# Linear attention and a squared-ReLU layer in one kernel: attention cut into smaller slices that are placed by running sums of two engines' work, and strip one's DMAs in another order

## The chip, the cores and the metric

The kernel runs on one core of a Trainium2 chip. The metric is device time in microseconds of that core, as a median over runs. Five engines work side by side, each through its own instructions in order: PE (TensorE, matrix products; its weight loads stand in the profile as an engine of their own, PEld), DVE (VectorE), ACT (ScalarE), POOL (GpSimd) and SP (SyncE), which here issues nearly all DMAs.

## The reference

```python
kv  = np.einsum('bhsd,bhse->bhde', k, v)        # b=8, h=8, s=576, d=64
out = np.einsum('bhsd,bhde->bhse', q, kv)
rms = np.sqrt(np.mean(out * out, axis=-1, keepdims=True) + 1e-06)
x   = (out / rms * g_norm)                      # to 4608 tokens x 512
h   = x @ w_in                                  # 512 -> 2048
y   = (np.maximum(h, 0.0) ** 2) @ w_out         # 2048 -> 512
```

Everything is float32. The two weight matrices arrive in 64 bits.

## The kernel before, in words

**Tokens.** The 4608 tokens are 36 tiles of 128, and nine strips of four tiles (512 tokens). Strips 0 and 1 have their own program, strips 2 to 8 share one. For each strip the feed-forward part has two stages. The up stage makes h and squares it, and the down stage multiplies by `w_out`. From strip 1 on, the products are made by the recursive seven-product scheme for 2x2 block matrices, one level deep in strip 1's up stage, two levels deep elsewhere. So each stage is a row of small matrix products (`up_small`, L1125; `small_products`, L941) whose results are added up by DVE, ACT and POOL.

**An up stage of strips 2 to 8** is 55 slots (`up_slot`, L1096). Seven outer products start seven slots apart, each with seven inner ones two slots apart, so from slot 7 on two of them interleave. An inner product fills one of the PSUM banks A, B, C (`BANK`); A takes four inner products one after the other, and each next one adds to what lies there. Before it does, ACT or DVE must have read the bank: L1155 (ACT copy), L1150 (DVE add), L1163 (ACT copy). The squaring is on ACT, two instructions (L1088, L1089). POOL makes sums of inputs (L288) and of results in SBUF (L1150). In slots 40 to 51 DVE also makes the first operands of the down stage (`leaf_steps`, L918).

**A down stage** is 14 steps. Each outer product there needs two weight blocks from DRAM, 0.75 MB from `w_out` (L831) and 1 MB from `w_deep` (L837). `stream` (L819) loads them in order of use into four equal buffers (`stream_pool`), and the buffers also hold `w_in_deep` blocks for the up stages (L825). Strips 0 and 1 write `w_deep` (L857, L863) and `w_in_deep` (L1051) themselves, from sums that DVE and POOL make; some of these sums lie in the same four buffers, others in the eight of `sum_pool`.

**Attention** for later strips is worked off between these products. `slices` (L630 to L690) is a list written out in order, and `attend` (L692) runs it up to a given place. For a pair of tiles it holds:

- `transposed_query` (L377): one DVE transpose of a query block (L383), for the last block of an odd batch a second one (L387); it also queues the loads of later queries.
- `key_value` (L414): PE products of k and v (L431), two ACT copies (L436, L437).
- `query` (L504): PE products (L467) for both tiles into one PSUM tile `x_ps`, of which there is one; two ACT squares (L476).
- `mean_roots` (L521): two DVE sums (L484), a scale and shift (L485), and ACT's root (L490).
- `normalized` (L527): four small DVE instructions (L495 to L499), and one DVE multiplication of 128x512 for each tile (L535).
- `squares_x` (L598): one DVE transpose for each tile (L602).
- `send_x` (L609): a store to DRAM (L611); `fetch_x` (L614) loads it back in the feature-major order, four DMAs (L618), at least six ticks of a planner's clock later.

**What sets the order.** The main loop (L1188 on) calls one feed-forward step, then perhaps one load, then `attend`. In strips 2 to 8 the list is spread evenly over the first 36 slots (`pace = 36`), one slice at a time and whole. Before strip s the loop calls `attend(ready[s])`, so that everything that strip s needs has been emitted. Loads of keys, of tiles and of queries wait in queues with due times on the planner's clock, which adds 1.2 for each up slot. A query is loaded only after its turn in the list has freed a buffer (three buffers).

**SP's queue** runs in program order. The built program gives its DMAs eight completion semaphores in turn, so a DMA also waits until the eighth before it has landed. A DMA that waits for an engine holds up all behind it.

**Strip 0's end and strip 1.** In strip 0's down stage SP stores `w_out` sums, loads the keys of batch 2 and the strip's last blocks. In strip 1's up stage (28 steps) POOL makes seven `w_in_deep` sums (`deep_sums_in`, L1044), DVE the last `w_deep` sums (in four parts, at steps 7, 9, 11 and 13), and the first four blocks of the down stage are loaded at steps 21, 22, 23 and 25. I call these b0 to b3, and the next ones b4 and so on.

Of the kernel before, what the change touches and what calls it, by code (L numbers as in the profile page):

```python
# [10 lines left out]
FP32 = mybir.dt.float32  # L11
# [3 lines left out]
AF = mybir.ActivationFunctionType  # L15
# [5 lines left out]
def kernel(  # L21
# [47 lines left out]
    NT = 4  # L69
# [4 lines left out]
    DEEP_UP = 2  # L74
    SQ = 32
    Q_ON_PE = 2
    X_ON_PE = 2
    EPS = 1e-6
    const = ctx.enter_context(tc.tile_pool(name="const", bufs=1))
# [207 lines left out]
    def minus(eng, out, a, b):  # L287
        eng.tensor_tensor(out=out, in0=a, in1=b, op=ALU.subtract)  # L288
# [125 lines left out]
    def key_value(b, *ps_of):  # L414
        while any(f == load and a[:2] == (b, p) or f == load_rest and a[0] == b for _, f, a in keys_due for p in ps_of):
            _, f, a = keys_due.popleft()
            f(*a)
        ps = apsum.tile([P, len(ps_of), D], FP32, name="kv_ps", tag="at")
        if (b, ps_of[0]) == (0, 0):
            keep_busy(ps[:, 0], 3)  # L420
            warm = apsum.tile([P, NT, P], FP32, name="x_ps", tag="first")[:, 0]
        half = slice(REST * (b % 2), REST * (b % 2 + 1))
        tiles = [[main.pop((n, b, p)) for n in "kv"] for p in ps_of]
        steps = [(i, c) for i in range(len(ps_of)) for c in range(C)] + [(i, C) for i in range(len(ps_of))]
        for i, c in steps:
            if (b, ps_of[i], c) == (0, 0, C):
                keep_busy(warm, 2)
            for h in range(2):
                at = (slice(None), h, c) if c < C else (half, 2 * ps_of[i] + h)
                a, w = (t[at] for t in (tiles[i] if c < C else (k_rest, v_rest)))  # L430
                nc.tensor.matmul(  # L431
                    ps[ts(h, D), i], lhsT=a, rhs=w, start=i == 0 and c == 0, stop=c == C, skip_group_check=True
                )
        at = (NP * b + ps_of[0]) % (2 * NP)
        d = kv_all[:, at : at + len(ps_of)]
        nc.scalar.copy(d[0:D, :, 0:D], ps[0:D])  # L436
        nc.scalar.copy(d[D:P, :, D:P], ps[D:P])  # L437
        for i, p in enumerate(ps_of):
            kvd[b, p] = d[:, i]
            if b < 2:  # L440
                if b == 1 and p == 0:
                    load_next()
            else:
                u = next(to_load, None)
                if u is not None:
                    keys_later(load, *u, nc.sync, "kv")
                if p == NP - 1 and b + 1 < B:
                    keys_later(load_rest, b + 1, nc.sync)

    by_head = lambda t: t.rearrange("p (h d) -> p h d", d=D)  # L450
# [37 lines left out]
    def root_of(ms, ps=None):  # L488
        r = ps if ps is not None else small.tile([P, 2, H], FP32, name="rms", tag="rms")[:, : ms.shape[1]]
        nc.scalar.activation(r, ms, AF.Sqrt)  # L490
        return r
# [23 lines left out]

    def roots_normalized(ns):
        parts, ms = queried.pop()
        queried.append((parts, (ms, root_of(ms))))
        normalized(ns)

    def mean_roots(ns):  # L521
        parts, sqs = queried.pop()
        ms = mean_of(sqs)
        r = apsum.tile([P, 2, H], FP32, name="root", tag="at")[:, : len(ns)]
        queried.append((parts, (ms, root_of(ms, r))))

    def normalized(ns):  # L527
        parts, means = queried.pop()
        r = inverse_root(*means)
        for i, n in enumerate(ns):  # L530
            x_n[n] = xn_pool.tile([P, d_model], FP32, name="x_n", tag="x_n")
            o = x_n[n].rearrange("p (q r d) -> p r q d", r=2, d=D)
            x = parts[i].rearrange("p r (q d) -> p r q d", d=D)
            w = r[:, i].rearrange("p (r q) -> p r q", r=2).unsqueeze(3).to_broadcast([P, 2, NP, D])
            nc.vector.tensor_tensor(out=o, in0=x, in1=w, op=ALU.mult)  # L535

    first = {}
    TAG_UP = "ABAC"
# [70 lines left out]
    def send_x(n):  # L609
        d = sent[n] = dram.tile([P, 4, NP, SQ], FP32, name="x_d", tag="x_d", bufs=2 * NT)  # L610
        nc.sync.dma_start(out=d, in_=squared.pop(n))  # L611
        tiles_due.append((clock[0] + 6, fetch_x, (n,)))

    def fetch_x(n):  # L614
        s, i = divmod(n, NT)
# [48 lines left out]
    T, K, last = transposed_query, key_value, query_pairs(1)[2]  # L664
    slices += [(query_means, (last,)), (K, (2, 0, 1)), (T, (2, 0)), (roots_normalized, (last,)), (T, (2, 1))]
    slices += [(T, (2, 2)), (features, (last[0],)), (T, (2, 3)), (K, (2, 2, 3))]
    for b in range(2, B):
        pairs = query_pairs(b)
        for i, pair in enumerate(pairs):
            left = len(pairs) - i  # L670
            more = b + 1 < B
            at = left + (b == 2)
            keys = (b + 1, *{2: (0, 1), 1: (2, 3)}[at]) if more and at < 3 else ()
            if i == 0 and b > 2:
                slices += [(T, (b, p)) for p in (2, 3)]
            if i == 0 and b == 3:
                slices.append((K, (3, 2, 3)))
            slices.append((query, (pair, *keys)))
            if more and left == 1:
                slices.append((T, (b + 1, 1)))  # L680
            slices.append((mean_roots, (pair,)))
            slices.append((normalized, (pair,)))
            if more and left == 2:
                slices.append((T, (b + 1, 0)))
            slices += [(squares_x, (n,)) for n in pair]
            for n in pair:
                slices.append((send_x, (n,)))
                if n % NT == NT - 1:
                    ready[n // NT] = len(slices)
    slice_at = [0]  # L690

    def attend(n):  # L692
        while slice_at[0] < min(n, len(slices)):
            fn, a = slices[slice_at[0]]
            fn(*a)
            slice_at[0] += 1

    def out_rows(n):

# [343 lines left out]

    def deep_sums_in(b):  # L1044

        t = stream_pool.tile([P, 4, FQ // 2, P], FP32, name="w_i", tag="w_blk")
        s1, s2, s4 = (t[:, i].rearrange("p f e -> p (f e)").rearrange("p (g e) -> p g e", g=2) for i in range(3))
        nc.gpsimd.tensor_tensor(out=s1, in0=w_half(b, 0, 1), in1=w_half(b, 1, 1), op=ALU.add)  # L1048
        minus(nc.gpsimd, s2, s1, w_half(b, 0, 0))
        minus(nc.gpsimd, s4, w_half(b, 1, 0), s2)  # L1050
        nc.sync.dma_start(  # L1051
            out=w_in_deep[b].rearrange("p n g e -> p n (g e)"), in_=t[:, 0:3].rearrange("p n f e -> p n (f e)")
        )

    def deep_differences_in(b):
# [132 lines left out]
    for s in range(N_STRIP):  # L1188
# [19 lines left out]
        goal, begun = ready.get(s + 1, len(slices)), slice_at[0]  # L1208
        if s >= DEEP_UP:
            goal = max(goal, min(ready[DEEP_UP] + (len(slices) - ready[DEEP_UP]) * (s - 1) // (N_STRIP - DEEP_UP - 1), len(slices)))  # L1210
        total, done = sum(w for w, _, _ in steps), 0
        for i, (w, fn, a) in enumerate(steps):
            if s == 0 and i < n_up:
# [32 lines left out]
            if s:  # L1246
                clock[0] += 3.2 if i >= n_up else 2.2 if s == DEEP else 1.2
                soon = tiles_due and tiles_due[0][2][0] // NT == s + 1
                if i == n_up + 10:
                    while tiles_due and tiles_due[0][2][0] // NT == s + 1:  # L1250
                        _, f, a = tiles_due.popleft()
                        f(*a)
                elif not due(keys_due) and not (soon and due(tiles_due)):
                    least = 2.1 if s == DEEP else 4.5 if i < n_up else 3.3
                    quiet = n_up * 2 // 3 < i < n_up + 3 or s == DEEP and i > n_up + 5
                    if not quiet and clock[0] >= dripped[0] + least:
                        dripped[0] = clock[0]
                        drip(True)
                pace = 25 if s == DEEP else 36
                attend(begun + (goal - begun) * min(i + 1, pace) // pace)  # L1260
                if s == DEEP and i in (7, 9, 11, 13):
                    if i == 7:
                        last_sums = store_deep_sums(*deep_due.popleft())
                    next(last_sums, None)
                if s == DEEP and i == n_up - 3:
                    leaf_sums(s, 4)
                if s == 1 and i in range(2, 23, 3):
                    deep_sums_in((1, 6, 5, 4, 0, 2, 3)[i // 3])
                if s == 1 and i in (21, 22, 23, 25):
                    stream()  # L1270
                continue
            if i == n_up:
# [15 lines left out]
                deque(store_deep_sums(*deep_due.popleft()), 0)  # L1288
            if i == n_up + 2:
                store_first(2)  # L1290
                for _ in range(2):
                    load_next(names="kv")
            if i == n_up + 3:
                load_rest(2, nc.sync)
            if 11 <= i < n_up:

# [31 lines left out]
```

## Time and profile before

| what | value |
|---|---|
| median of 3 runs (lowest, highest) | 898.01 us (897.0, 902.7) |
| the profiled execution: its own time | 897.09 us |
| the profiled execution: its span | 895.0 us |
| granted TensorE clock | 0.999 |
| DMA: bytes moved, mean rate | 235.71 MB, 263 GB/s |

The span runs from the first to the last instruction; 2.1 us of the time lie around it. The ends of matmuls are modelled in this profile, so PE looks busy even when the next product starts late. I therefore read the starts of the products, and the idle time before weight loads (PEld): in a stage of small products, weight loads follow each other without a gap unless the next product has to wait. A timeline row shows start, length, engine, line, what is written and read, how many instructions it merges, and in brackets the idle time before it and who ended it.

In the time line of the two-level stages, one product of the scheme is a row of eight PE instructions, and the next such row starts 0.89 us later. That is also the length of one up slot. One whole outer product of a down stage takes 6.25 us.

### The profile page before, as it was taken

The page shows a single profiled execution, that of the slowest core. Times are in us where ns is not written, and L with a number is a line of the kernel's source. Part 1 is how long each engine was busy: PE and PEld are TensorE (multiplying, and loading weights), DVE is VectorE, ACT ScalarE, POOL GpSimd, SP SyncE. Part 2 cuts the span into 40 slices and gives each one's busy share as a digit, 9 for nine tenths or more (in the row PEclk, how much of TensorE's full clock was granted, in tenths as well). Part 3 has the DMA queues.
Part 4 walks back from the last instruction along what each step waited for, and adds up shares of the span by engine and source line. Part 5 has one row for each costly group of instructions (what it writes and reads, how often), then busy time and mean ns, then how long its engine had stood idle before and what let it go on. Part 6 is the DMA issues. An engine that isn't in the chain of part 4 may idle for free.

```text
span 895.0 us, 20696 instructions
## 1 busy us (share of the span) xinstructions
PE 879.5 (98%) x8296; PEld 822.0 (92%) x8296; DVE 730.9 (82%) x1256; ACT 315.3 (35%) x622; POOL 306.7 (34%) x315
## 2 busy tenths in 40 slices
PE   8999999999999999999999999999999999999998
PEld 7445888889999999999999999999999999999998
DVE  4999988878778986798689966985899778875886
ACT  5898242220027302640255023801271027102710
POOL 0000005700448233731373035604460447044700
PEclk9999999999999999999999999999999999999999
DMA  9998998999988798799886989798748965884384
GB/s 322 317 300 266 290 361 246 260 303 336 309 208 280 261 324 234 189 331 325 249 231 242 320 247 239 244 293 299 218 142 295 302 205 164 301 299 155 127 321 177
DMA packets 169663, 235.71 MB, mean 263 GB/s; under 512 B 79456, under 2 KB 134240, under 8 KB 161248
## 3 DMA queue, kind: packets, MB, share of 16 engines
q1 hardware_dynamic: 169408, 234.40, 81.2%
q8 instruction: 65, 1.06, 0.5%
q14 instruction: 30, 0.25, 0.1%
q10 hardware_dynamic: 160, 0.00, 0.0%
HBM read 197.66 MB, written 36.70 MB: 262 GB/s over the span
## 4 chain that ended last, share of the span: by engine, by line
PE 75%; DVE 12%; DMA 8%; issue 2%; SPq 2%; ACT 1%; DVEq 0%; POOL 0%; POOLq 0%; ACTq 0%
PE ps_B L950 21%; PE ps_A L1138 16%; PE ps_A L950 16%; PE ps_B L1138 8%; PE ps_C L1138 4%; PE ps_A L733 3%; DMA w_blk<-w_deep 2%; DMA w_deep<-w_t 2%; PE kv_ps L431 2%; DVE w_c L268 2%; PE x_ps L467 1%; DVE w_t L288 1%; PE ps_B L733 1%; DMA raw<-in_moe_w_in_dram 1%; DVE wt L288 1%
## 5 line engine op out<-in xcount | busy, mean ns | idle before, releaser
L950 PE MATMUL ps_B<-w_blk,g_s 128*128 128x128 f32 x1024 | 126.2, 275 | 0.0
L950 PEld LDWEIGHTS ps_B<-w_blk,g_s 128*128 128x128 f32 x1024 | 120.0, 192 | 0.2
L1138 PE MATMUL ps_A<-x_l,w_in 128*128 128x128 f32 x784 | 104.1, 276 | 0.0
L950 PE MATMUL ps_B<-w_blk,gt 128*128 128x128 f32 x768 | 97.6, 275 | 2.9 <-DMA w_blk<-w_out 1.7
L288 POOL TENSOR_TENSOR x_l<-xT 128x256 f32<-128x256 f32 x21 | 15.7, 749 | 241.8 <-PE ps_A L950 241.8
L1138 PEld LDWEIGHTS ps_A<-x_l,w_in 128*128 128x128 f32 x784 | 95.4, 192 | 0.5 <-DVE gt L1150 0.2
L950 PEld LDWEIGHTS ps_B<-w_blk,gt 128*128 128x128 f32 x768 | 91.4, 192 | 3.7 <-issue 2.1
L950 PE MATMUL ps_A<-w_blk,g_s 128*128 128x128 f32 x768 | 93.6, 275 | 0.0
L950 PEld LDWEIGHTS ps_A<-w_blk,g_s 128*128 128x128 f32 x768 | 89.6, 192 | 0.0
L1150 POOL TENSOR_TENSOR snap<-snap,gt 128x512 f32<-128x512 f32 x35 | 46.6, 1331 | 119.3 <-ACT snap L1155 49.0
L1155 ACT COPY snap<-ps_A 128x512 f32<-128x512 f32 x63 | 36.7, 582 | 133.6 <-PE ps_A L1138 111.0
L965 DVE TENSOR_TENSOR o_sb<-o_sb,ps_B 128x256 f32<-128x256 f32 (+1 forms) x128 | 49.5, 387 | 33.0 <-ACT o_sb L966 25.9
L1088 ACT ACTIVATE gt<-gt 128x512 f32<-128x512 f32 x112 | 69.6, 622 | 18.0 <-DVE gt L1150 18.0
L950 PE MATMUL ps_A<-w_blk,gt 128*128 128x128 f32 x576 | 72.3, 275 | 0.0
L1089 ACT ACTIVATE gt<-gt 128x512 f32<-128x512 f32 x112 | 70.6, 631 | 3.6
L950 PEld LDWEIGHTS ps_A<-w_blk,gt 128*128 128x128 f32 x576 | 68.2, 192 | 0.0
L1150 POOL TENSOR_TENSOR gt<-gt,snap 128x512 f32<-128x512 f32 x42 | 52.6, 1276 | 23.4 <-DVE snap L1150 23.4
L1048 POOL TENSOR_TENSOR w_i<-w_in 128x512 f32<-128x512 f32 x7 | 9.8, 1396 | 147.2 <-DMA q<-in_q_dram 141.6
L288 DVE TENSOR_TENSOR gt<-gt 128x2048 f32<-128x2048 f32 (+1 forms) x29 | 59.7, 2063 | 0.0
L966 ACT COPY o_sb<-ps_A 128x128 f32<-128x128 f32 x24 | 6.4, 265 | 145.8 <-PE ps_A L950 145.8
L1138 PE MATMUL ps_A<-x_l,w_blk 128*128 128x128 f32 x392 | 52.2, 276 | 1.3 <-issue 1.2
L1138 PE MATMUL ps_B<-x_l,w_blk 128*128 128x128 f32 x392 | 52.0, 276 | 0.0
(180 smaller groups left out, 1805.5 us busy)
## 6 DMA issues: line engine op xcount, KB each, us to landing
w_blk<-w_deep SPq DMA_DIRECT2D x56, 1024.0 KB, 6.9
w_blk<-w_out SPq DMA_DIRECT2D x56, 768.0 KB, 5.9
w_blk<-w_in_deep SPq DMA_DIRECT2D x49, 768.0 KB, 5.2
raw<-in_moe_w_in_dram SPq DMA_DIRECT2D x16, 512.0 KB, 7.6
raw<-in_moe_w_out_dram SPq DMA_DIRECT2D x16, 512.0 KB, 6.8
k<-in_k_dram SPq DMA_DIRECT2D x29, 256.0 KB, 4.6
v<-in_v_dram SPq DMA_DIRECT2D x29, 256.0 KB, 4.9
x_d<-x_q SPq DMA_DIRECT2D x27, 256.0 KB, 5.0
```

What stands on the lines that cost most here:

```text
L268: yield nc.vector.scalar_tensor_tensor(out=ci, in0=high, scalar=-(2**30), in1=ci, op0=ALU.bitwise_and, op1=ALU.bitwise_or)
L288: eng.tensor_tensor(out=out, in0=a, in1=b, op=ALU.subtract)
L431: nc.tensor.matmul(ps[ts(h, D), i], lhsT=a, rhs=w, start=i == 0 and c == 0, stop=c == C, skip_group_check=True)
L733: nc.tensor.matmul(bank[BANK[p]][:, i, :], lhsT=lhsT(k), rhs=rhs(k), start=p in (1, 5, 2) and i == 0 and k == 0, stop=k == n - 1, skip_gro ...
L950: nc.tensor.matmul(chain[c][x][:, i, :], lhsT=a[:, f, :], rhs=w[:, f, :], start=x not in opened[c] and f == 0, stop=f == FQ // 2 - 1, skip ...
L965: add = lambda out, a, b: nc.vector.tensor_tensor(out=out, in0=a, in1=b, op=ALU.add)
L1048: nc.gpsimd.tensor_tensor(out=s1, in0=w_half(b, 0, 1), in1=w_half(b, 1, 1), op=ALU.add)
L1088: nc.scalar.activation(o, o, AF.Relu)
L1089: nc.scalar.activation(o, o, AF.Square)
L1138: nc.tensor.matmul(ps[:, i, :], lhsT=w, rhs=rhs, start=j in (1, 2, 5) and i == 0, stop=True, skip_group_check=True)
L1150: add = lambda eng, out, a, b: eng.tensor_tensor(out=out, in0=a, in1=b, op=ALU.add)
L1155: nc.scalar.copy(t, ps)
```

## The change

1. **Smaller slices from batch 3 on.** `mean_roots` and `normalized` are cut up: `mean` (one tile's sum on DVE), `root` (ACT), `inverse` (four small DVE instructions), and `scaled_heads`. The last takes the place of DVE's multiplication at L535: for half of a tile's heads it gives ACT four multiplications of 128x64, each with a scale per partition. Batch 2 keeps the old slices.
2. **Placement by running sums.** In strips 2 to 8 `attend_between` takes the place of the even spread. It keeps a sum for DVE and one for ACT. Each slot takes 0.9 us off and adds what the feed-forward slot costs these engines; a slice is run only if its engine's sum stays at most 1.6, with no second slice for one engine in a slot, until the list must hurry to be done by slot 38.
3. **A strip's goal** is moved to the nearest end of a pair of tiles, and a query block's transposes stand elsewhere in the list.
4. **Strip 0's end:** the last-but-one block's load and the first output store go ahead of four key loads; the remaining key loads go behind a store of four parts.
5. **Strip 1:** the `w_deep` sums at steps 3, 4, 7 and 9; b0 to b3 at steps 17, 20, 21 and 23; one of the POOL sums lies in `sum_pool` and is stored in three DMAs; tiles 9 to 11 are fetched at least 18 ticks after their store, and query loads of batch 3 wait for the down stage.
6. **Keys' rest rows** from batch 5 on are loaded one step earlier.

```diff
+    BEHIND = 1.6
...
-                if p == NP - 1 and b + 1 < B:
+                if p == (1 if b > 3 else NP - 1) and b + 1 < B:
                     keys_later(load_rest, b + 1, nc.sync)
...
+    def scaled_heads(ns, i, r):
+        o, x, w = place_of(ns, i)
+        for p in range(NP):
+            nc.scalar.activation(o[:, r, p], x[:, r, p], AF.Copy, scale=w[:, r, p : p + 1])
+        if i == len(ns) - 1 and r:
+            queried.pop()
...
-        tiles_due.append((clock[0] + 6, fetch_x, (n,)))
+        tiles_due.append((clock[0] + (6 if n >= DEEP_UP * NT + NT else 18), fetch_x, (n,)))
...
+            slices += [(mean, (pair, t)) for t in range(len(pair))]
+            slices += [(root, (pair,)), (inverse, (pair,))]
+            heads = [(scaled_heads, (pair, t, r)) for t in range(len(pair)) for r in range(2)]
+            slices += heads[:3]
+            for t, n in enumerate(pair):
+                slices += [(squares_x, (n,)), (send_x, (n,))]
+                if n % NT == NT - 1:
+                    ready[n // NT] = len(slices)
+                if t == 0:
+                    slices += heads[3:]
+            pair_ends.append(len(slices))
...
+    ON_DVE = {mean: 0.7, inverse: 0.9, squares_x: 0.67, transposed_query: 0.67}
+    ON_ACT = {query: 1.1, root: 0.2, scaled_heads: 0.9}
...
+    def attend_between(slot, begun, goal, late, first, last):
+
+        for on, cost in feed_forward_cost(slot).items():
+            behind[on] = max(behind[on] - 0.9, 0.0) + cost
+        if slot == 0:
+            rest_at[0], keys_at[0] = -9, -99
+        used, most = set(), begun + -(-(goal - begun) * min(max(slot + 1 - late, 0), first) // first)
+        while slice_at[0] < most:
+            fn, a = slices[slice_at[0]]
+            on, cost = ("dve", ON_DVE[fn]) if fn in ON_DVE else ("act", ON_ACT.get(fn, 0.0))
+            if fn == transposed_query and a[1] == NP - 1 and a[0] % 2:
+                cost, rest_at[0] = 2 * cost, slot
+            if fn == query and (0 <= slot - rest_at[0] < 3 or len(a) > 1 and 0 <= slot - keys_at[0] < 12):
+                return
+            if fn != send_x:
+                left = sum(f != send_x for f, _ in slices[slice_at[0] : goal])
+                if used and (on in used or fn in (root, inverse) or used & {root, inverse}):
+                    return
+                if left <= last - slot and behind[on] + cost > BEHIND:
+                    return
+                used |= {on, fn}
...
+            behind[on] += cost
+            attend(slice_at[0] + 1)
...
-        t = stream_pool.tile([P, 4, FQ // 2, P], FP32, name="w_i", tag="w_blk")
+        if b == 0:
+            t = [sum_pool.tile([P, FQ // 2, P], FP32, name=f"w_i{i}", tag="sum") for i in range(3)]
...
+            if s > DEEP_UP:
+                goal = min(pair_ends, key=lambda end: abs(end - goal))
...
-                    quiet = n_up * 2 // 3 < i < n_up + 3 or s == DEEP and i > n_up + 5
+                    quiet = n_up * 2 // 3 < i < n_up + 3 or s == DEEP and i > n_up + 9
+                    quiet = quiet or s == DEEP and i < n_up and drips and drips[0][0] == load_q_rest
...
-                pace = 25 if s == DEEP else 36
-                attend(begun + (goal - begun) * min(i + 1, pace) // pace)
-                if s == DEEP and i in (7, 9, 11, 13):
-                    if i == 7:
+                if s == DEEP:
+                    attend(begun + (goal - begun) * min(i + 1, 25) // 25)
+                elif i < n_up:
+                    attend_between(i, begun, goal, *(2, 34) if s == DEEP_UP else (0, 27), 38)
+                if s == DEEP and i in (3, 4, 7, 9):
+                    if i == 3:
...
-                if s == 1 and i in (21, 22, 23, 25):
+                if s == 1 and i in (17, 20, 21, 23):
                     stream()
...
             if i == n_up + 2:
                 store_first(2)
+            if i == n_up + 3:
                 for _ in range(2):
                     load_next(names="kv")
-            if i == n_up + 3:
+            if i == n_up + 6:
                 load_rest(2, nc.sync)
```

In the built program PE has the same instructions as before, and only some products of attention stand one to four products earlier or later; POOL has the same in the same order. DVE loses 23 multiplications (tiles 13 to 35), ACT gains 184, and SP has two more DMAs.

## The prediction

> **What bounds the kernel now.** I read the busy line first.
>
> ```profile
> PE 879.5 (98%) x8296; PEld 822.0 (92%) x8296; DVE 730.9 (82%) x1256; ACT 315.3 (35%) x622; POOL 306.7 (34%) x315
> ```
>
> PE does the work that sets the end, and the built program gives it the same instructions as before. So the change can win only what PE stands still. The busy share hides that, since ends of matmuls are modelled. I therefore took the waits of the weight loads, by whom they waited for; the columns are total us, times, longest.
>
> ```profile
> PEld ps_B L1138 <- DVE snap L1150: 2.7, 5, 0.9
> PEld ps_B L950 <- issue: 2.1, 1, 2.1
> ...
> PEld ps_A L1138 <- issue: 1.8, 3, 1.4
> PEld ps_B L950 <- DMA w_blk<-w_deep: 1.6, 2, 0.8
> ...
> PEld ps_B L733 <- DVE w_in L288: 1.2, 1, 1.2
> ...
> PEld ps_A L733 <- DVE o_sb L899: 0.7, 1, 0.7
> ...
> PEld ps_A L1138 <- DVE gt L1150: 0.6, 2, 0.4
> PEld x_ps L467 <- DVE qT_rest L387: 0.5, 1, 0.5
> ```
>
> The other rows of that view belong to the opening (lines 375 to 580 and 774) or to attention's first products in strips 0 and 1 (under 0.8 each), which stay. The rows shown are the ledger: L733 is strips 0 and 1, L950 the down stages, L1138 and L467 strips 2 to 8. They add to 1.9 + 3.7 + 5.6 = 11.2 us, 1.2% of the time. More than that is not to be had.
>
> Then the time line, to see what each stall is. The 2.1 and one of the w_deep waits stand at the start of strip 1's down stage:
>
> ```profile
> 198.38 1.86 PEld L950 LDWEIGHTS ps_B<-w_blk,gt 128*128 128x128 f32 x16 [2.11 <-issue]
> 200.16 0.97 PEld L950 LDWEIGHTS ps_B<-w_blk,g_s 128*128 128x128 f32 x8
> 201.91 0.74 PEld L950 LDWEIGHTS ps_B<-w_blk,gt 128*128 128x128 f32 x6 [0.77 <-DMA w_blk<-w_deep]
> ```
>
> PE had its last up product by 196.67 and waited for block b0; three products later it waited for b1. In DVE's time line of strip 5's up stage (start, length) the other kind is seen:
>
> ```profile
> 558.46 1.29 DVE L535 TENSOR_TENSOR x_n<-x_ps,newton 128x512 f32<-128x512 f32 x2
> 559.66 0.68 DVE L1150 TENSOR_TENSOR gt<-ps_C,snap 128x512 f32<-128x512 f32 x1
> 560.26 0.68 DVE L1150 TENSOR_TENSOR snap<-ps_B,snap 128x512 f32<-128x512 f32 x1
> 560.86 0.70 DVE L383 STREAM_TRANSPOSE qT<-q 128x512 f32<-128x512 f32 x1
> 561.49 0.67 DVE L602 STREAM_TRANSPOSE x_q<-x_n 128x512 f32<-128x512 f32 x1
> 562.08 1.25 DVE L1150 TENSOR_TENSOR gt<-ps_A,gt 128x512 f32<-128x512 f32 x2
> 563.25 0.67 DVE L1150 TENSOR_TENSOR snap<-ps_B,gt 128x512 f32<-128x512 f32 x1
> 563.85 0.69 DVE L602 STREAM_TRANSPOSE x_q<-x_n 128x512 f32<-128x512 f32 x1
> ```
>
> DVE runs without a pause. The multiplications and transposes of attention stand in the same queue as the adds of L1150 that must read a bank before PE may go on, and PE's weight loads at 560.40 and 563.98 come 0.37 and 0.83 us late.
>
> **The change, part by part.** *Strip 0's end.* The block that PE lacked at 123.97 to 125.22 (strip 0's sixth product) left SP at 117.56, behind four key loads of 256 KB that left from 112.39 on. It now goes before them, some 5 us earlier, with 1 MB less ahead of it; even with half of that it lands in time. Of the 1.25 us idle 0.2 is the ordinary distance of weight loads of 256 columns (rows of L733), so 1.0 is won. The 0.67 at 132.66 (0.4 over the ordinary) is DVE's add at L899, late because DVE waited until 129.38 for a store of w_deep that left at 121.17; two rest loads no longer stand ahead of that store. I take 0.3. What is moved back has room: the keys left SP by 117.5, the rest loads by 121, and both are used from 145.8 on (L431); 8 us later they still have over 10. Sum 1.3, between 0 and 1.4.
>
> *Strip 1.* b0 left SP at 191.38, and between the POOL store at 183.15 and it stood two small rest-query loads, four key loads, the last POOL sum's store and one tile's four fetches. At step 17 it leaves after the POOL store at 183.15, so about 183.6. With the median 5.9 us of such loads it lands near 190, 6 us before PE needs it. b1 follows the last POOL store (187.43) at 187.9; with the 7.9 us that it took before it lands at 195.8, and is needed at 196.6 + 2.7 = 199.3 (24 weight loads of 0.112). Both waits go: 2.1 + 0.8. The third, 0.8 at 227.81, was a 1 MB load that took 9.5 us from 218.29 (chain of waits) while four query loads in 128-byte pieces left beside it; those now leave some 12 us later (steps 36 and 37 instead of 32 and 33) and only tiny ones stand there. I take it as gone as well. Ledger 3.7, less 0.2 of ordinary distance: 3.5.
>
> Against it: b3 now gets b0's buffer (the built program's addresses say so; before, it got the last POOL sum's). So it can leave only after PE has read b0, at 199.3. It is needed after b2's products, at 196.6 + 6.25 + 2.7 = 205.5. The DMAs have nothing else from 195 on; alone, 0.75 MB takes about 5 us (b4 took 4.8 before), so b3 lands at 204.4, just in time; with the median of 6.9 it would be 206.2. Behind it in SP wait tile 11's store and eight fetches, then b4. The eighth-before rule makes the seventh fetch wait for b3's landing, so b4 leaves near 205.5 (206.87 before), lands near 210.3, and is needed at 209.1: 1.2 us late, my value. The bounds are 0 and 3.5 (each later block of the stage is late in turn, and the gain is gone). What hides the moved fetches and rest queries is time: they are used at the end of strip 1 and in strip 2's slot 4, over 20 us later. The w_deep sums four steps earlier free four of the eight sum buffers for the POOL sum that moved there; were they late, POOL would wait, and behind it both last POOL sums, their stores and b0. They leave near 163 instead of 171.85, the sum is made near 175: covered by about 4 us. Net 3.5 - 1.2 = 2.3.
>
> *Attention in strips 2 to 7.* Of the 5.6 us of the ledger (with two small rows 5.8), 0.6 at 294.11 is not attention's (there DVE makes the down stage's operands), nor are some small ones; 4.4 are stalls with attention's DVE work just ahead of the late add: 1.4 and 0.2 near 533 to 535, 0.4, 0.8 and 0.2 near 560 to 565, 0.9 at 636.64, 0.5 at 645.21. DVE is spared 23 multiplications, 23 x 0.686 = 15.8 us, which by itself is worth nothing where PE doesn't wait. The spacing is worth more: at most one DVE slice per slot, none while DVE is over 1.6 us behind. A bank's next product stands four slots after the first one in the interleaved part, so 2.7 us lie between for a read of 0.68; 1.6 behind and 0.68 fit. I let 4.0 of the 4.4 go.
>
> ACT's new work has no row of its own. The nearest:
>
> ```profile
> L405 ACT COPY qT<-t_ps 128x512 f32<-128x512 f32 x8 | 4.7, 589 | 4.9 <-PE t_ps L403 4.6 <-PE t_ps L400 0.3
> L570 ACT ACTIVATE xT<-xt_ps,g_col 128x512 f32<-128x512 f32 x4 | 2.7, 686 | 2.0 <-PE xt_ps L569 2.0
> L437 ACT COPY kv_all<-kv_ps 64x64 f32<-64x64 f32 x8 | 1.7, 207 | 0.1
> ```
>
> 64 columns cost 207 ns, a scale per partition adds 686 - 589 = 97, together 304. Independent instructions overlap: L1089 at 562.22 runs 0.63, the next starts at 562.76, 0.09 earlier than its end. So four take 4 x 0.214 + 0.09 = 0.95 us, and 46 slices 43.7 us. [...] The trace says which engine has it to give: between 242.5 and 290 ACT is busy 22.2 of 47.5 us, DVE 37.2; eight slices more make ACT 29.8. I count the 43.7 us as hidden. Uncovered they would cost all of it.
>
> The new waits: ACT's slice waits for `inverse` on DVE, and behind it in ACT's queue stand copies of banks (L1155) that PE waits for. DVE may be 1.6 behind when `inverse` is done, ACT's slice starts up to 0.7 after its slot, and three such slices follow each other, so ACT can be some 2.3 us late, more than the 2.7 - 0.58 of a copy. That is a few tenths in some of the 13 pairs; `root` on ACT waits less than before. Bounds: 0 and 13 x 0.95 = 12; I take 1.0, since ACT already waited 33.5 us for L485 in 15 goes (waits of all engines), up to 4.9, and no weight-load row names an ACT copy of L1155. Net 3.0. Moved transposes find their queries loaded 8 us or more before, the key products likewise; I count 0. SP's extra issues (two of 0.4) lie in its idle time.
>
> **Sum.** 1.3 + 2.3 + 3.0 = 6.6 off 897.09 is 890.5. The median of the runs stands 0.9 above the profiled execution, their lowest 0.1 below; I carry half, 0.5, and say 891.0.
>
> **The rivals.** *Strip one gives its gain back:* PE starts sooner and meets the same DMA stream, which moves 321 GB/s between 205 and 240 at 94% of the engines' time. For: nearly every block of that stage landed just before its use. Against: b0 to b2 are there before the stage begins. Time 891.0 + 2.3 = 893.3. *The slices bring as much waiting as they take away:* stalls of 0.23 us in each of 13 pairs, 894.0; with twice that 897.0. *All of it works:* no late block, no new waits, all of the 4.4: 891.0 - 1.2 - 1.0 - 0.4 = 888.4; the ledger's floor, all 11.2 off, is 886.4. *Slower:* in the ACT queue of strips 2 to 7 the multiplications make the bank copies late. If ACT is late by one slice in each pair, 13 x 0.95 = 12.4 us are added: 903.4. It decides from 6.6/46 = 0.14 us of stall a slice on. For it speaks the in-order queue, against it the ACT share and the missing L1155 row.
>
> **How the numbers follow.** A stall saved passes to the end one for one, as PE is never idle for another reason. Chances: the forecast 0.55 (own range 889.2 to 892.8), strip one lost 0.14, slices net nothing 0.14, all works 0.12, slower 0.05. The range 887.5 to 896.0 takes in these and leaves out the slower case, the doubled waits and the floor, about 0.14. About 1% is what a measurement here can tell from no change: 889.0 and 907.0. Below 889.0 lie most of the all-works case and a fifth of the forecast, 0.22; above 907.0 the worst half of the slower one, 0.02; between them 0.76.
>
> **What would show it.** Right: no weight-load wait at the sixth product of strip 0 nor at the down stage's first products in strip 1; L1150 rows behind L1138 under 2 us; ACT near 359 us, DVE near 715. A wait of L950 for w_blk some 9 us into strip 1's down stage shows the b3 or b4 cost; rows of PEld L1138 behind ACT L1155 show the slower rival. I am wrong if waits of L1138 grow, or if the DMA waits only move to later blocks.

## The result and the profile after

The changed kernel takes 892.02 us (median; 889.28 to 894.95), the kernel before 898.15 us on the same chip: a ratio of 0.9923, 95% interval 0.9901 to 0.9945, so 0.8% faster. The forecast was 891.0. The profiled execution took 889.28 us, its span is 887.3. It is the fastest run of this kernel: the median stands 2.7 us above it, not 0.5 as I carried.

The busy line of the page after:

```profile
PE 876.6 (99%) x8296; PEld 821.8 (93%) x8296; DVE 721.4 (81%) x1233; ACT 352.3 (40%) x806; POOL 307.3 (35%) x315
```

ACT has its 184 new instructions and 37 us more work (I expected 44), DVE 23 instructions fewer but only 9.5 us less work (I expected 15.8). The waits of weight loads after (total us, times, longest), the rows that answer to the ledger:

```profile
PEld ps_B L1052 <- DMA w_blk<-w_out: 1.7, 1, 1.7
...
PEld ps_A L835 <- DVE o_sb L1001: 0.8, 1, 0.8
...
PEld xt_ps L632 <- PE ps_A L835: 0.7, 1, 0.7
...
PEld ps_B L1248 <- DVE snap L1260: 0.6, 1, 0.6
PEld ps_A L1248 <- ACT snap L1265: 0.5, 1, 0.5
```

(L835 is L733 of before, L1052 is L950, L1248 is L1138, L1260 and L1265 are L1150 and L1155.) Of attention's waits one of 0.5 is left, behind ACT; the 0.6 was there before. In strip 5's up stage, DVE's time line now reads:

```profile
554.32 1.29 DVE L1260 TENSOR_TENSOR gt<-ps_A,gt 128x512 f32<-128x512 f32 x2 [0.83 <-PE ps_A L1248]
555.52 0.68 DVE L1260 TENSOR_TENSOR snap<-ps_B,gt 128x512 f32<-128x512 f32 x1
556.16 0.69 DVE L1260 TENSOR_TENSOR snap<-ps_A,gt 128x512 f32<-128x512 f32 x1
556.77 0.70 DVE L639 STREAM_TRANSPOSE x_q<-x_n 128x512 f32<-128x512 f32 x1
```

DVE waits for PE there, not PE for DVE, and one piece of attention (L639) stands between the adds, where before the pieces of L535, L383 and L602 stood close together. At the start of strip 1's down stage, PEld's time line has the waits for b0 and b1 no more, but a new one for b4, 14.4 us into the stage:

```profile
195.95 1.97 PEld L1052 LDWEIGHTS ps_B<-w_blk,gt 128*128 128x128 f32 x16
...
205.88 2.76 PEld L1052 LDWEIGHTS ps_A<-w_blk,g_s 128*128 128x128 f32 x24
210.33 1.86 PEld L1052 LDWEIGHTS ps_B<-w_blk,gt 128*128 128x128 f32 x16 [1.69 <-DMA w_blk<-w_out]
```

To see which stage gained, I take the start of the same PE product in two profiles. Its shift against the profile of before, at 99.5, 159.7, 196.3, 245.0, 262.0 and 735.3 us of that profile, gives the gain of each stage (negative is earlier; the up stage of strip 1 gave 0.0 in every kernel and is left out). Time and ratio are those of the timed runs against the kernel before on the same chip (the ratio is made from all runs of both, so it isn't exactly that of the medians); kernels are named and explained in the next section.

| kernel | opening | strip 0's end | strip 1's down stage | strip 2's start | strips 2 to 8 | median us | ratio, 95% |
|---|---|---|---|---|---|---|---|
| changed | +0.2 | -0.5 | -2.0 | -0.3 | -5.1 | 892.0 | 0.9923 (0.9901 to 0.9945) |
| e1_order_only | +0.2 | +2.7 | -0.2 | 0.0 | +0.4 | 899.2 | 1.0005 (0.9989 to 1.0022) |
| e2_slices_only | +0.6 | +0.5 | +0.3 | -0.3 | -5.0 | 891.8 | 0.9926 (0.9899 to 0.9953) |
| e3_even_small | +0.6 | -0.5 | +0.1 | -0.3 | -1.8 | 895.4 | 0.9961 (0.9945 to 0.9978) |
| e4_dve_scaled | +0.4 | +0.1 | +2.5 | -0.3 | -5.9 | 893.6 | 0.9926 (0.9899 to 0.9953) |
| e5_b3_early | +0.5 | 0.0 | -2.9 | -0.3 | -5.0 | 890.7 | 0.9919 (0.9899 to 0.9940) |
| e6_even_guard | +0.5 | +0.3 | +0.4 | -0.3 | -5.3 | 892.1 | 0.9942 (0.9920 to 0.9964) |
| e7_act_twice | +0.4 | -0.4 | -1.0 | -0.3 | +15.2 | 912.6 | 1.0156 (1.0135 to 1.0178) |
| e8_b3_dve | +0.5 | -0.2 | -1.6 | -0.3 | -4.4 | 890.3 | 0.9909 (0.9891 to 0.9928) |
| e9_even_dve | +1.1 | +0.4 | +0.6 | -0.3 | -3.3 | 896.4 | 0.9973 (0.9957 to 0.9989) |
| e10_quiet | 0.0 | -1.0 | -3.7 | +5.6 | -6.2 | 892.0 | 0.9929 (0.9906 to 0.9951) |
| e11_before_again | +1.0 | -0.9 | -0.4 | 0.0 | -0.1 | (897.0, once) | - |
| e12_quiet_late | 0.0 | -0.3 | -3.7 | -0.3 | -3.9 | 889.7 | 0.9920 (0.9898 to 0.9942) |

Read alone, the first row bears the forecast out: strips 0 and 1 gave 2.5 us, attention 5.3. The other rows say that the first half of this is luck of one profile.

### The profile page after: what moved, and what is told of

Its sections match the earlier page's. It is cut to its first block, busy times and chain, and to the rows that moved or that the text cites. A ratio compares the mean times of both kernels' runs of the same rounds, so it can differ in the third digit from the quotient of the medians.

```text
span 887.3 us, 20876 instructions
## 1 busy us (share of the span) xinstructions
PE 876.6 (99%) x8296; PEld 821.8 (93%) x8296; DVE 721.4 (81%) x1233; ACT 352.3 (40%) x806; POOL 307.3 (35%) x315
## 4 chain that ended last, share of the span: by engine, by line
PE 82%; DVE 10%; DMA 3%; ACT 3%; issue 2%; SPq 0%; POOL 0%; DVEq 0%; POOLq 0%; ACTq 0%
PE ps_B L1052 22%; PE ps_A L1248 19%; PE ps_A L1052 16%; PE ps_B L1248 9%; PE ps_C L1248 5%; PE ps_A L835 4%; PE kv_ps L432 2%; PE x_ps L468 2%; DVE w_c L269 2%; PE ps_B L835 1%; DMA w_deep<-w_t 1%; DVE w_t L289 1%; DVE wt L289 1%; PE ps_C L835 1%; DVE w_c L263 1%
## 5 line engine op out<-in xcount | busy, mean ns | idle before, releaser
L1052 PE MATMUL ps_B<-w_blk,g_s 128*128 128x128 f32 x1024 | 126.1, 275 | 0.0
L1052 PEld LDWEIGHTS ps_B<-w_blk,g_s 128*128 128x128 f32 x1024 | 120.0, 192 | 0.1
L1248 PE MATMUL ps_A<-x_l,w_in 128*128 128x128 f32 x784 | 103.8, 275 | 0.3 <-ACT snap L1265 0.3
L1052 PE MATMUL ps_B<-w_blk,gt 128*128 128x128 f32 x768 | 97.5, 275 | 1.5 <-DMA w_blk<-w_out 1.5
L1248 PEld LDWEIGHTS ps_A<-x_l,w_in 128*128 128x128 f32 x784 | 95.4, 192 | 0.6 <-ACT snap L1265 0.5
L1052 PE MATMUL ps_A<-w_blk,g_s 128*128 128x128 f32 x768 | 93.6, 275 | 0.0
L1052 PEld LDWEIGHTS ps_B<-w_blk,gt 128*128 128x128 f32 x768 | 91.5, 192 | 1.7 <-DMA w_blk<-w_out 1.7
L1052 PEld LDWEIGHTS ps_A<-w_blk,g_s 128*128 128x128 f32 x768 | 89.6, 192 | 0.0
L1260 POOL TENSOR_TENSOR snap<-snap,gt 128x512 f32<-128x512 f32 x35 | 45.9, 1310 | 119.2 <-ACT snap L1265 103.7
L1265 ACT COPY snap<-ps_A 128x512 f32<-128x512 f32 x63 | 36.9, 585 | 109.5 <-PE ps_A L1248 96.2
L1052 PE MATMUL ps_A<-w_blk,gt 128*128 128x128 f32 x576 | 72.2, 275 | 0.0
L1052 PEld LDWEIGHTS ps_A<-w_blk,gt 128*128 128x128 f32 x576 | 68.2, 192 | 0.0
L1154 POOL TENSOR_TENSOR w_i<-w_in 128x512 f32<-128x512 f32 x7 | 10.7, 1524 | 148.1 <-DMA q<-in_q_dram 140.8
L1260 POOL TENSOR_TENSOR gt<-gt,snap 128x512 f32<-128x512 f32 x42 | 52.4, 1277 | 17.6 <-DVE snap L1260 17.4
L1248 PE MATMUL ps_B<-x_l,w_blk 128*128 128x128 f32 x392 | 52.1, 276 | 0.0
L1248 PE MATMUL ps_A<-x_l,w_blk 128*128 128x128 f32 x392 | 51.9, 275 | 0.0
```

What stands on the lines that cost most here:

```text
L1052: nc.tensor.matmul(chain[c][x][:, i, :], lhsT=a[:, f, :], rhs=w[:, f, :], start=x not in opened[c] and f == 0, stop=f == FQ // 2 - 1, skip ...
L1248: nc.tensor.matmul(ps[:, i, :], lhsT=w, rhs=rhs, start=j in (1, 2, 5) and i == 0, stop=True, skip_group_check=True)
L1260: add = lambda eng, out, a, b: eng.tensor_tensor(out=out, in0=a, in1=b, op=ALU.add)
L1265: nc.scalar.copy(t, ps)
```

## The experiments

**The two halves of the change, one at a time.** e1_order_only is the kernel before with parts 4 and 5 of the change, e2_slices_only with the rest:

```diff
-                if s == 1 and i in (21, 22, 23, 25):
+                if s == 1 and i in (17, 20, 21, 23):   # e1, beside the other edits of parts 4 and 5
...
-                attend(begun + (goal - begun) * min(i + 1, pace) // pace)
+                    attend_between(i, begun, goal, *(2, 34) if s == DEEP_UP else (0, 27), 38)   # e2, beside the new list
```

> The kernel before with only the new order of DMAs and sums in strips 0 and 1; attention as before. My theory (the parts add up, and strips 0 and 1 bring about 2 of the 7.6 us): 896 us, some 2 us under the kernel before; in the profile no wait at strip 0's sixth product and at the start of strip 1's down stage, one of 1.5 to 1.7 us at its third outer product (block b4), and attention's stalls in strips 2 to 7 still 4 to 5 us. Rival (strip 1 only passes its gain on because the smaller slices follow): no gain left at the end of strip 2, 898 us.

> The kernel before with only the smaller slices, their placement by running sums and the earlier rest rows; strips 0 and 1 as before. My theory: strips 2 to 7 lose 5 of their 5.4 us of stalls, so 893 us; waits of 1.9 to 2.1 for b0, 0.7 for b1 and 0.8 for a later block in strip 1 stay. Rival (the forecast on record): 3.0 us, 895 us. Rival (the slices net nothing): 898 us.

Measured: the order of DMAs alone 1.0005, nothing; the slices alone 0.9926, the whole gain. My theory for e1 (2 us) fell. The rival's wording fell too: it is not that a gain is lost in strip 2, none leaves strip 1.

**Where strip 1's gain goes.** Seven profiles have the changed strip 1 (the changed kernel, e1, e3, e4, e6, e7, e9). In its down stage they stand at -2.0, -0.2, +0.1, +2.5, +0.4, -1.0 and +0.6: a mean of +0.1. The three with the old one (before, e2, e11) stand at 0.0, +0.3 and -0.4. In all seven the waits for b0 and b1 are gone and b4 is waited for, by 1.5 to 2.5 us; in five of them blocks at 230 to 243 us come late too, by 0.8 to 3.4 in all. For b4 the DMAs tell why. The window from 196 to 200 us (PE, PEld, DVE, ACT and POOL busy, granted clock, DMA share, GB/s) in the kernel before and in the changed one:

```profile
196.00:200.00 4.00, 2.26 (x18) 1.86 (x17) 3.90 (x7) 1.23 (x2) 0.00 (x0) 1.00 1.05 281
```

```profile
196.00:200.00 4.00, 4.00 (x37) 3.97 (x36) 3.90 (x7) 1.23 (x2) 0.00 (x0) 1.00 0.17 57
```

From 200 to 210 us the DMA share is 0.84 and 0.97. Before, PE stood still in this window and the DMAs worked; now PE works and the DMAs stand still, since b3 waits for b0's buffer and everything waits behind b3 in SP's queue. The row of that wait, between 195 and 200 us (L939 is `stream`'s load, L1052 the product that reads b0):

```profile
SPq L939 <- PE ps_B L1052: 11.3, 1, 11.3
```

In e5_b3_early the last POOL sum lies in the sum buffers instead of the fifth; the rotation then gives b3 a buffer that is free early:

```diff
-        if b == 0:
+        if b == 3:
             t = [sum_pool.tile([P, FQ // 2, P], FP32, name=f"w_i{i}", tag="sum") for i in range(3)]
```

> The changed kernel, but the last of the seven POOL sums lies in the sum buffers in place of the fifth, so that block b3 gets a buffer that is free early instead of b0's. Theory (strip 1 gives its gain back because the DMAs stand still from 196 to 199 us while b3 waits for b0's buffer): b3 leaves at 187 to 188 us, the DMAs move over 200 GB/s from 196 to 200 us in place of 57, the waits for b4 (1.7 to 2.5 us in the profiles so far) and for the blocks near 240 us (0 to 1.9) are gone or under 1 us in all, and the time is 889 to 890 us. Rival (the stage is bound by what the DMAs have to move until 245 us, whatever the order): the waits come at other blocks, still 2.5 us or more in the stage, and the time is 892 us.

The same window in e5:

```profile
196.00:200.00 4.00, 4.00 (x33) 3.87 (x32) 3.89 (x7) 1.23 (x2) 0.00 (x0) 1.00 1.00 419
```

SP's rows for b3, in the changed kernel and in e5 (start of the issue, its length):

```profile
199.04 0.32 SPq L939 DMA_DIRECT2D w_blk<-w_deep  x1
```

```profile
191.35 0.32 SPq L939 DMA_DIRECT2D w_blk<-w_deep  x1
```

b3 leaves 7.7 us earlier (not at 187: b1 and b2, ahead of it in SP's queue, left at 189.75 and 190.47), b4 isn't waited for, and of the waits one of 0.7 is left near 237 us. None of the four kernels with this edit (e5, e8, e10, e12) waits for b4. They stand at -2.9, -1.6, -3.7 and -3.7 in the stage: a mean of -3.0 beside +0.1, but e10 and e12 have a further edit there (below); e5 and e8 alone give -2.3. So without the hole the stage keeps most of its gain. The medians bear it out only weakly: e5 and the changed kernel have intervals that overlap.

**What it is in the slices.** Three kernels change how attention is cut and placed, and e9_even_dve joins e4's and e6's edits:

```diff
+                    attend(begun + (goal - begun) * min(i + 1, 36) // 36)                  # e3: even spread
+            if fn == query and 0 <= slot - rest_at[0] < 3:                                 # e6: e3 with this one rule
+                return
+            heads = [(scaled, (pair, t)) for t in range(len(pair))]                        # e4: DVE's multiplication, sums kept
```

> The changed kernel with its small slices, but spread evenly over 36 slots in place of the running sums. If the placement by sums brings the gain, stalls behind L1248 come back, 3 to 5 us in strips 2 to 7, and the time is 895 to 897 us. If smaller slices and DVE's relief bring it, stalls stay under 1 us and the time is 892 us.

> The changed kernel with DVE's one multiplication of 128x512 for each tile in place of ACT's four and four, placed by the same running sums (one slice of 0.69 for each tile). DVE is then busy 15.8 us more and ACT 41 us less. If the placement brings the gain, stalls in strips 2 to 7 stay under 1.5 us and the time is 892 to 893 us. If the move to ACT brings it, they are 3 us or more and the time is 895 us or more. If ACT's new work costs something, the time is under 891 us.

> The changed kernel with its small slices spread evenly over 36 slots, and one rule only: a query waits until three slots after the two transposes of the last query block. Theory (small slices take away DVE's stalls, and of the placement only this rule counts): the two waits of 1.65 us for qT_rest are gone, strips 2 to 7 stall under 1 us, and the time is that of the changed kernel, 892 us. Rival (the running sums are needed): stalls of over 2 us in strips 2 to 7, 894 to 895 us.

> The changed kernel with small slices, DVE's one multiplication a tile in place of ACT's, and the even spread with the one rule for the query. If cutting attention up is all that counts, strips 2 to 7 stall under 1 us as with the other three arrangements, and the time is 892 us. If the running sums or the move to ACT are needed, one of them at least, DVE's queue runs full again: stalls behind DVE L1260 of 2 us or more in strips 2 to 7, and 894 us or more.

e3 loses 3.3 of attention's 5.1 us, but not to DVE's adds: no wait behind L1260 of 0.2 or more is left in strips 2 to 7. Two waits of 1.65 us are for `qT_rest`, where a query directly follows its transposes, as PE's row of the first one says:

```profile
451.44 0.34 PE L468 MATMUL x_ps<-kv_all,qT_rest 64*64 64x64 f32 x8 [1.49 <-DVE qT_rest L388]
```

e6 holds such a query back for three slots, and has 5.3 again. e4 gives the multiplications back to DVE under the same sums and has 5.9, with no wait behind DVE nor ACT. So the running sums can go, and so can the move to ACT. e9 drops both. It has no wait behind DVE either, so what takes DVE's stalls away is the small pieces, with one rule for the query. All these kernels also have parts 3 and 6 of the change, which were not tried apart from them.

But e9's time, 896.4, is 4 us above e6's, and I expected 892: with both gone, over half of the gain is gone too. What it loses are loads. Its profile shows 1.7 us of waiting for keys and 1.1 for a block at 610:

```profile
550.48 0.58 PEld L432 LDWEIGHTS kv_ps<-v,k 128*64 128x64 f32 x16 [1.71 <-issue]
```

That v left SP at 544.22, once the eighth DMA before it, one of a tile's fetches, had landed at 544.17, and landed itself at 550.37. In e6, where the fetches stand behind the keys' loads, v left at 541.63 and landed at 547.32. So the place of attention's slices also sets the order of the DMAs. That is one profile; how often this order is late in the other 21 runs was not seen.

**What ACT has to give.** e7_act_twice makes each small multiplication twice, writing the same values again:

```diff
-        for p in range(NP):
+        for p in (0, 1, 2, 3, 0, 1, 2, 3):
             nc.scalar.activation(o[:, r, p], x[:, r, p], AF.Copy, scale=w[:, r, p : p + 1])
```

> The changed kernel with each of ACT's 184 small multiplications made twice (the second writes the same values again), placed as before; ACT is busy some 40 us more. If ACT's work is hidden with room to spare, under 1 us is added: 892 to 893 us. If it sits near the edge, as the forecast's slower rival says (from 0.14 us a slice on the change is a loss), copies of banks come late: rows of PEld L1248 behind ACT L1265 of some us, 896 us or more.

ACT's row of the multiplications, changed kernel and e7 (busy us, mean ns, idle before):

```profile
L570 ACT ACTIVATE x_n<-x_ps,newton 128x64 f32<-128x64 f32 x184 | 40.8, 338 | 7.3 <-DVE newton L500 7.2
```

```profile
L570 ACT ACTIVATE x_n<-x_ps,newton 128x64 f32<-128x64 f32 x368 | 79.7, 396 | 7.2 <-DVE newton L500 7.2
```

38.9 us more on ACT cost 20.3 us of time in strips 2 to 8 (+15.2 against -5.1). The forecast's slower rival is seen at work, in e7's time lines of ACT and of PEld:

```profile
571.32 1.73 ACT L570 ACTIVATE x_n<-x_ps,newton 128x64 f32<-128x64 f32 x8
572.90 0.68 ACT L1198 ACTIVATE gt<-gt 128x512 f32<-128x512 f32 x1
573.61 0.63 ACT L1199 ACTIVATE gt<-gt 128x512 f32<-128x512 f32 x1
574.14 0.57 ACT L1265 COPY snap<-ps_A 128x512 f32<-128x512 f32 x1
```

```profile
574.76 1.78 PEld L1248 LDWEIGHTS ps_A<-x_l,w_in 128*128 128x128 f32 x8 [3.34 <-ACT snap L1265]
```

The bank's copy stands behind attention and two squares, and PE waits 3.3 us. Such waits of 0.3 us or more add to 15.1 us in e7's strips 2 to 8 (1.1 in the changed kernel), and after two of them the granted clock was at half for 10.2 us in all, about 5 us more by estimate (half of that time; see the last section). The first 41 us of work on ACT cost 0.5 in the changed kernel's profile, the next 39 cost 20: the first filled what was free.

**Putting it together.** e8_b3_dve joins e5 and e4; e10_quiet also moves four query loads in 128-byte pieces out of the end of strip 1's down stage, where part 5 of the change had put them; e12_quiet_late also lets attention of strip 2 begin five slots later.

```diff
-                    quiet = n_up * 2 // 3 < i < n_up + 3 or s == DEEP and i > n_up + 9
+                    quiet = n_up * 2 // 3 < i < n_up + 3 or s == DEEP and i > n_up + 7          # e10, e12
...
-                    attend_between(i, begun, goal, *(2, 34) if s == DEEP_UP else (0, 27), 38)
+                    attend_between(i, begun, goal, *(7, 31) if s == DEEP_UP else (0, 27), 38)   # e12
```

> The earlier b3 and DVE's multiplication together. If both theories hold, no stall of 0.2 us or more is left in strips 2 to 7 and under 1 us of waits in strip 1's down stage: 889 us, the fastest of all. If the earlier b3 brings nothing: 892 us.

> The kernel with the earlier b3 and DVE's multiplication, and four query loads in 128-byte pieces moved out of the end of strip 1's down stage. Theory (these pieces make the 1 MB block late that PE waited for by 0.7 and 1.7 us near 237 us): that wait is under 0.5 us and the time is 889 us. Rival (the stage's DMAs are full of blocks, stores and fetches anyway): the wait stays over 0.6 us, 890 us.

> The quiet end of strip 1 as before, and attention in strip 2 begins seven slots into the strip (6.3 us) in place of two, so that the first query no longer meets loads that are not there. Theory (the four query loads moved out cost 3.5 us of waiting for qT_rest and 1.2 us of a lower clock after it, and nothing else): strip 1's gain of 4.7 us is kept through strip 2, no wait of over 0.5 us at 245 to 260 us, profiled time 886 to 887 us, median 888 us, under every kernel so far. Rival (attention then has too few slots in strip 2 and hurries): new stalls in strip 2 of 2 us or more, 890 us or more.

e8 gives 890.3 us: attention as expected, but blocks still late at 237 (1.8), 293 (0.9) and 504 us (0.7). The block at 237 took 10.7 us from issue to landing with the four query loads beside it (9.4 in e5), and 7.5 in e10 without them. In e10 its wait is gone and strip 1 gains 3.7, all lost again at the start of strip 2. Its time lines of DVE and PEld there:

```profile
247.52 0.71 DVE L384 STREAM_TRANSPOSE qT<-q 128x512 f32<-128x512 f32 x1 [6.68 <-DMA q<-in_q_dram]
```

```profile
248.88 0.30 PEld L468 LDWEIGHTS x_ps<-kv_all,qT_rest 64*64 64x64 f32 x8 [3.52 <-DVE qT_rest L388]
```

The loads moved out are what the first query needs. e12 lets it come later and keeps the 3.7: its profiled execution took 888.9 us, the lowest of all, but its median is 889.7, not 888; in the profile other blocks came late (0.8 at 290, 1.3 at 600 to 604 us). e5, e8 and e12 can't be told apart by these runs; each median is under the changed kernel's.

**The kernel before again**, for how far a profile repeats:

> The kernel before once more, for a second profile of it. If the first profile was typical, the waits in strip 1's down stage add to 3.4 us again and attention's stalls to the same 4.9 us; engine waits repeat to 0.1 us, DMA waits need not.

Attention's waits repeat to 0.02 us each. The DMA waits don't: 0.4 at strip 0's sixth product (1.0 in the first profile), 2.3 and 0.8 at the start of strip 1's down stage (1.9 and 0.7), and none at 227 us (0.8). Together they make 4.0 us (4.9).

## Why the prediction was right, and where it was not

That the time was within 1.0 us of the forecast is luck in good part, since two errors nearly cancel: 1.3 + 2.3 for strips 0 and 1 came out as nothing, and 3.0 for attention as 5.3 in the profile (5.1, and 0.3 at strip 2's start). 5.3 is within what the timed runs allow for the whole, 4.9 to 8.9 us.

- *What bounds the kernel*: right. PE does the same work, its floor didn't move, and the gain is below the 11.2 us of the ledger. What the ledger could not say is how far its DMA half differs from one execution to the next: by 0.9 us in sum between the two profiles of this kernel, and by 4.5 us in the stage over the seven that share the changed strip 1. It was read from one. "A stall saved passes to the end one for one" also leaves out the granted clock: 0.57 in the 4 us after a stall of 2.4 us in e6 (last section).
- *Strip 0, 1.3*: wrong, 0 (eleven profiles with the new order: mean 0.0, or -0.2 without e1, where the granted clock was 0.55 from 135 to 138 us; three with the old: -0.1). The first half holds: the wait at the sixth product is under 0.25 us in all eleven. The step that failed is "I take 0.3" for L899. The store of w_deep left SP at 118.13 instead of 121.17, but landed at 128.50 instead of 129.29: it took 10.4 us in place of 8.1, with a DMA share of 0.95 from 100 to 125 us (0.92 before). Why it took longer was not tested. DVE's rows behind it, before and after:

```profile
129.38 0.69 DVE L288 TENSOR_TENSOR w_t<-w_blk 128x512 f32<-128x512 f32 x1 [0.77 <-DMA w_deep<-w_t]
```

```profile
128.59 0.69 DVE L289 TENSOR_TENSOR w_t<-w_blk 128x512 f32<-128x512 f32 x1 [0.46 <-DMA w_deep<-w_t]
```

DVE gains 0.8 us, PE had gained 1.0, so PE waits longer for the add (0.6 in the changed kernel, 0.6 to 2.3 in nine of the ten others, 0.2 to 0.4 with the old order). The rest goes at 155 us, in a place that the prediction didn't look at: PE now reaches a transposition 0.4 us before DVE has its `x_n` (the row of `xt_ps` above, 0.4 to 0.5 in all profiles with the new order but e1's, where PE was late anyway).
- *Strip 1, 3.5 - 1.2*: the mechanism was right and a term too small. b3 was forecast to leave at 199.3 and did at 199.04 (it is a 1 MB block, not 0.75 as I wrote, and took 5.3 us); b4 was forecast to leave at 205.5 and land at 210.3, and did at 205.45 and 210.28. But PE needed it at 208.6, not at 209.1, so b4 was late by 1.7, and the step "1.2 us late, my value" stopped at the first late block. Over the seven profiles b4 was late by 2.0 on average and the blocks from 230 to 243 us by 1.4, together 3.4 of the 3.5 to be won, near my upper bound. The later ones are not the hole's alone: e5 and e8 have no hole and still wait 0.7 and 1.8 there. "I take it as gone as well", of the third wait, is a step that failed: the query loads that left beside a block at 218 us now leave beside one at 229 us, and the wait can come there; in e10 and e12, without them, it is gone. The rival "strip one gives its gain back" is what happened. Its mechanism as I put it, a full stream, is half of it: e5 shows that the stream has room when b3 doesn't wait.
- *Attention's stalls, 4.0 of 4.4*: right in place, all of them went, with the small rows that I hadn't counted. "The spacing is worth more" was wrong as a reason: e6 has the same gain without running sums. DVE's relief of 15.8 us was forecast to be worth nothing, and e4 shows it. Only the two together can't be dropped, for another reason than DVE's stalls (e9).
- *ACT's new work*: a slice took 40.8 / 46 = 0.89 us, forecast 0.95 from the rows of before. Multiplications on DVE are the better choice here by a little: e4 stands 0.8 ahead in strips 2 to 8, of which 0.5 is the missing wait behind ACT. The timed runs can't show that.
- *New waits, 1.0*: one, of 0.5 us, at 562 us. "I count the 43.7 us as hidden" holds, but e7 shows how little is left beyond it.

## What to carry to other kernels

Strip 1's down stage, fed by DMAs, gained from an earlier start only when the stream behind it started earlier too (-2.3 us in e5 and e8, +0.1 over the seven profiles where b3 waited): look at the DMA share just after the wait that you remove, and at whose buffer the next load in the queue waits for. In DVE's queue, on which PE's progress depends, short pieces took the stalls away here (no wait behind L1260 of 0.2 us or more in strips 2 to 7 of e3), whether work moved to another engine or not (e9); before giving work to another engine, double that work once to see how much is free. Waits for DMAs differed between the two profiles of the kernel before by 0.9 us in sum, as much as a small change brings, so its parts are timed one at a time, or read from several profiles.

## What the runs showed of the hardware

A long wait of PE was followed by a lower granted clock in some profiles and not in others. After 2.4 us at b4 in e6 the granted clock was 0.57 for the next 4 us (window 212 to 216 us, the column ahead of the last two):

```profile
212.00:216.00 4.00, 3.93 (x20) 3.93 (x21) 3.23 (x6) 0.00 (x0) 0.00 (x0) 0.57 1.03 424
```

In e4 PE waited 2.5 us for the same block and kept its clock (same window):

```profile
212.00:216.00 4.00, 4.00 (x36) 4.00 (x37) 3.61 (x6) 0.00 (x0) 0.00 (x0) 1.00 1.01 416
```

It was also lower in e1 after 2.5 us at 131 us (0.91 from 131 to 135 us, 0.55 from 135 to 138; about 1.7 of its +2.7 by estimate, 4 x 0.09 + 3 x 0.45), in e7 after 3.3 us at 571 us (0.50 from 575 to 580) and in e10 after 3.5 us at 245 us (0.50 from 249 to 252), and not after 2.3 us in e11 (1.00 from 194 to 202). From 575 to 580 us PE has 24 instructions in e7 at 0.50, and 47 in e4 at 1.00. Two more places of e7, with PE's busy time as the second figure:

```profile
662.49:665.91 3.42, 1.56 (x14) 1.37 (x13) 1.54 (x3) 3.39 (x13) 2.52 (x3) 1.00 0.66 216
665.91:669.32 3.41, 3.41 (x19) 3.41 (x18) 2.74 (x5) 3.31 (x7) 1.86 (x4) 0.50 0.51 159
737.59:741.00 3.41, 1.92 (x18) 1.73 (x16) 1.89 (x3) 3.41 (x19) 0.34 (x1) 1.00 0.11 43
741.00:744.42 3.42, 2.08 (x45) 2.01 (x46) 1.97 (x3) 2.14 (x9) 0.00 (x0) 1.00 0.25 94
```

At the first PE was idle for 1.86 us, and the next 3.41 us had half the clock. At the second it was idle for 2.84 us in all, and the clock was 1.00 throughout. So the length of the wait alone does not tell whether the clock goes with it; what decides was not shown.

The mean granted clock also parts the timed runs. Of 82 timed runs of the kernel before that went with the experiments, 35 had a mean granted clock of 0.998 or less (3.41 us at half the clock, as in e7 above, take 0.0019 off the mean by estimate, 3.41 / 2 / 895) and took 899.7 us on average, the other 47 897.4. The same holds for e9: 898.0 for 11 of its 22 runs, 894.3 for the others. It was one run in ten of the changed kernel, and none of e5 and e8. So some of the timed gain, about 0.7 us by estimate (35/82 of 1.7 us, e1's loss above), may be clock that is no longer lost.
